# A chunked mLSTM with two gated feed-forward layers: the first 24 feed-forward steps in an order that the program fixes on all engines

## The chip, the core and the metric

The kernel runs on one core of a Trainium2 chip. Such a core has a matrix engine (TensorE, PE in the rows; its weight loads are the rows PEld), three engines for elementwise work (VectorE = DVE, ScalarE = ACT, GpSimd = POOL), and SyncE (SP), which here only starts DMA transfers. Each engine works through its own queue in order and waits for others by semaphores. The metric is device time in microseconds of one launch. All times of single instructions come from one profiled execution.

## The reference

```python
# attention: B=2, H=8, S=768, D=40; a recurrence over t
m_new = max(f[t] + m, i[t])
C = exp(f[t] + m - m_new) * C + exp(i[t] - m_new) * outer(v[t], k[t])
n = exp(f[t] + m - m_new) * n + exp(i[t] - m_new) * k[t]
y[t] = sigmoid(o_gate[t]) * (C @ q[t]) / max(|n . q[t]|, 1)

# layer 1, tokens = 1536, d_model = 320, d_ff = 1536
x = (sigmoid(x @ w_gate) * (x @ w_val)) @ w_out
# layer 2
xn = x / sqrt(mean(x*x) + 1e-6) * rms_g
out = (silu(xn @ w_gate2) * (xn @ w_val2)) @ w_out2
```

All inputs are float32.

## The kernel before

The sequence is cut into six chunks of 128 time steps. A chunk holds 128 tokens of each of the two batch entries, that is 256 tokens of layer 1. Within a chunk the recurrence is written as matrix products (scores `a_s`, decayed scores `a_p`, their product with v `a_pv`, the part from the state of the chunk before `a_inter`, the new state `a_u`, normalisation `a_h`); `a_x` transposes the result into `xT`, the moving operand of layer 1. Each of these is called once per batch entry or per four heads (`qd`).

The hidden width 1536 of a feed-forward layer is cut into 12 tiles `f` of 128. A step of layer 1, `moe(c, f)`, makes gate and value of one tile for one chunk: 16 products of 128x256 into one PSUM bank of tag "g", a sigmoid on ACT, a product `h` on DVE. `moe_out(c, f)` multiplies `h` with the output weights and adds to the banks "o". For the chunks 0 and 1 (`NAT = 2`) these are two float32 products (the trace shows each of them as two, hence "x4"); from chunk 2 on, `h` and the output weights are split into a high and a low part, and a step takes six products. Steps are numbered from 0 here: the list `seq` has 24 steps for the chunks 0 and 1 (which chunk comes when is the string `ORDER`), then 12 for each of the chunks 2 to 5, then the steps of layer 2.

A tile of weights arrives as 64-bit words by one DMA (`load_w`) and is converted: `conv_w` does two ACT instructions (a scaling of the upper words, line 167, and a shift of the top byte, line 178), `conv_1` and `conv_2` do three DVE instructions (lines 190 and 202). `split_w` makes the high and low parts: three ACT copies (line 209), then subtractions (`sub`, line 205): the large one of 128x512 either as one DVE instruction (`go=1`) or as two POOL instructions of 128x256, a small one on POOL, and a small one of 64x128 on DVE, the function `low`. A step needs all of these parts of its tile. The output weights of the chunks 2 and later are split by `split_o`: an ACT copy, and a subtraction on POOL or DVE.

What sets the order: the code is written step by step, but only what stands before step `NPIN = 8` is pinned, which means that each engine keeps the order in which the program was written (`pin`, line 764). `early(i)` holds what is written behind the first four steps. From step 8 on, the framework's scheduler orders the instructions of each engine by its own estimates of when each can start, so that an instruction written for a later step may stand ahead of one that the current step needs. The conversions of tiles 4 to 11, the loads, the attention of chunk 2 (`C2S` gives its places, `EV2` the distances within) and `split_o` go through the table `ev`, which names the step at which each is written. Three products of a zero tile, `busy(idle, ...)` in line 753, stand ahead of step 0 only to give PE something to do.

Of the kernel before, what the change touches and what calls it, by code (L numbers as in the profile page):

```python
# [7 lines left out]
F32 = mybir.dt.float32  # L8
# [6 lines left out]
AF = mybir.ActivationFunctionType  # L15
# [52 lines left out]
@with_exitstack  # L68
def mlstm_moe_kernel(ctx, tc, gate_if, gate_s, qk, qg, tok, w1, w2, rms_g, cst, out):
    nc = tc.nc  # L70
    pool = lambda name, bufs=1, **kw: ctx.enter_context(tc.tile_pool(name=name, bufs=bufs, **kw))
    const = pool("const")
    wp = pool("w")
# [70 lines left out]
    def conv_w(f, tag="wc", lo_dve=0, both=True, sg_act=0, dve=False):  # L144

        bytes_ = wraw[f].bitcast(U8).rearrange("p (n b) -> p n b", b=8)
        top = bytes_[:, :, 3]  # L150
# [451 lines left out]
    seq += [(2, c, f) for c in range(NC // 2) for f in range(NF)]  # L602
    pos = {k: i for i, k in enumerate(seq)}

    for c in range(2, NC):
        for b in range(B):
            s0 = C2S[b] if c == 2 else 12 * (c - 1) + 6 * b + S0
            qa, qb = 2 * b, 2 * b + 1
            if True:
                at(s0 - 4, load_qk, c, b)  # L610
                at(s0 - 3, load_tok, c, b)
            d = EV2
            assert s0 + d[12] <= pos[1, c, 0]
# [12 lines left out]
            at(s0 + d[7], a_k, c, qb)
# [6 lines left out]
    at(10, lambda: nc.gpsimd.tensor_scalar(out=rmsg, in0=rmsg, scalar1=2.0 ** -16, scalar2=None, op0=ALU.mult))  # L633
    assert max(X0 + X1) <= 12
    for c in range(NC):
        for b in range(B):
            i = 2 * (c % 2) + b
            at(n1 - 12 + X0[i] if c < 2 else n1 + 12 * (c // 2 - 1) + X1[i], to_xT2w, c // 2, i, 2 * c + b)
    for f in range(NF):
        t = pos[1, 0, f]  # L640
        at(NF * NAT + f - 1, split_o, f, O1[f])
        if f >= 6:
            at(t - LW, load_w, w1, f)
        if f >= 4:
# [230 lines left out]
    def early(i):

        if i == 0:
            split_w(1, 1)
            a_s(1, 1, ("o2", "o3"))
            for qd in range(4):  # L880
                a_k(1, qd)
            a_p(1, 0)
            a_p(1, 1)
            conv_w(2)
        elif i == 1:
            a_inter(1, 0)
            load_qg(1, 1)
            load_w(w1, 4)
            split_w(2, 1)
            a_p(1, 2, p2.tile([128, 4, L], F32, tag="ft", name="p"))  # L890
            a_p(1, 3, p2.tile([128, 4, L], F32, tag="ft", name="p"))
            a_o(1, 0)
            a_o(1, 1)
            a_pv(1, 0)
            a_pv(1, 1)
            a_u(1, 0)
            conv_w(3)
            load_w(w1, 5)
        elif i == 2:
            a_h(1, 0)  # L900
            split_w(3, 1)
            a_inter(1, 1, "o2")
            a_pv(1, 2, "o3")
            a_pv(1, 3, "o3")
            a_u(1, 1, "a")
            a_x(1, 0, "a")
            a_h(1, 1)
        elif i == 3:
            a_x(1, 1, "o2")

    assert min(ev) >= 0, min(ev)
    for i in range(len(seq) + SKEW):
# [9 lines left out]
        if 0 <= i < len(seq):  # L922
# [3 lines left out]
            if i < NPIN:  # L926
                early(i)
        while 0 <= i and done < len(seq) and done <= i - (SKEW if seq[done][0] == 1 and seq[done][1] >= NAT else 1):
            layer, c, f = seq[done]
            (moe_out if layer == 1 else moe2_out)(c, f)  # L930
            done += 1
# [84 lines left out]
```

## Time and profile before

| what | before |
|---|---|
| median of 3 runs | 504.8 us (503.46 to 505.42) |
| the profiled execution | 505.04 us, span 503.2 us, mean granted clock 0.989 |
| PE busy | 485.2 us (96%) |
| DVE, ACT, POOL busy | 303.1, 222.5, 210.0 us |
| window 24 to 54 us | PE busy 26.82 of 30, DVE 26.99 |
| window 54 to 131 us | PE busy 71.57 of 77, DVE 53.99, ACT 37.72, POOL 35.48 |

Step 0 starts at 26.26 us and step 23 ends at about 131 us; the rest of the span holds the steps 24 to 107. PE's busy time counts a product that runs at half clock as busy as any other, so the granted clock has to be read beside it (column PEclk, 1.00 is the full 2.4 GHz, 0.50 is 1.2 GHz). A row of the timeline gives start, duration, engine, line, operation, output and inputs; neighbouring instructions of one kind are merged ("x16"), and since products overlap, the pace is read from the start of one row to the start of the next. In brackets stands the idle time ahead of an instruction and what ended it.

### The profile page before, as it was taken

The page shows a single profiled execution, that of the slowest core. Times are in us where ns is not written, and L with a number is a line of the kernel's source. Part 1 is how long each engine was busy: PE and PEld are TensorE (multiplying, and loading weights), DVE is VectorE, ACT ScalarE, POOL GpSimd, SP SyncE. Part 2 cuts the span into 40 slices and gives each one's busy share as a digit, 9 for nine tenths or more (in the row PEclk, how much of TensorE's full clock was granted, in tenths as well). Part 3 has the DMA queues.
Part 4 walks back from the last instruction along what each step waited for, and adds up shares of the span by engine and source line. Part 5 has one row for each costly group of instructions (what it writes and reads, how often), then busy time and mean ns, then how long its engine had stood idle before and what let it go on. Part 6 is the DMA issues. An engine that isn't in the chain of part 4 may idle for free.

```text
span 503.2 us, 8423 instructions
## 1 busy us (share of the span) xinstructions
PE 485.2 (96%) x3264; PEld 434.8 (86%) x3266; DVE 303.1 (60%) x564; ACT 222.5 (44%) x485; POOL 210.0 (42%) x238
## 2 busy tenths in 40 slices
PE   8988989899999999999999889999999999999997
PEld 5877869678899999999999778988888888888886
DVE  6899594993679586596779986622352222432223
ACT  3764653553434543455578666322252222432122
POOL 2733385451256364354249996332213222132221
PEclk9998989899999999999999999999999999999999
DMA  7763736721123232023444412000010000100001
GB/s 233 250 208 116 239 108 251 253 98 40 61 64 84 80 85 82 1 67 108 158 158 156 158 66 92 1 0 1 0 54 0 1 0 1 53 2 0 1 0 52
DMA packets 12557, 42.58 MB, mean 85 GB/s; under 512 B 1590, under 2 KB 4870, under 8 KB 12518
## 3 DMA queue, kind: packets, MB, share of 16 engines
q1 hardware_dynamic: 12278, 41.84, 24.8%
q8 instruction: 25, 0.41, 0.3%
q10 hardware_dynamic: 240, 0.22, 0.2%
q14 instruction: 14, 0.11, 0.1%
HBM read 40.05 MB, written 2.00 MB: 84 GB/s over the span
## 4 chain that ended last, share of the span: by engine, by line
PE 65%; DVE 5%; DMA 4%; POOL 3%; issue 2%; ACT 1%; POOLq 0%; ACTq 0%
PE g L804 13%; PE a L804 13%; PE o L856 12%; PE g L786 11%; PE o L831 6%; PE o L786 4%; DMA wraw<-in_w_dram 4%; PE o L828 2%; POOL h L205 1%; POOL wg L205 1%; DVE wg L205 1%; PE a L392 1%; PE a L457 1%; PE a L438 1%; PE a L470 1%
## 5 line engine op out<-in xcount | busy, mean ns | idle before, releaser
L786 PE MATMUL g<-xT,wg 128*128 128x256 f32 x912 | 131.2, 293 | 1.1 <-ACT gb L338 0.4
L786 PEld LDWEIGHTS g<-xT,wg 128*128 128x128 f32 x912 | 118.2, 193 | 7.2 <-issue 1.7
L205 POOL TENSOR_TENSOR ft<-p,fb 128x512 fp32r<-128x512 f32 x35 | 45.2, 1293 | 130.6 <-ACT fb L813 130.5
L807 DVE TENSOR_TENSOR p<-p,g 128x512 f32<-128x512 f32 x36 | 24.5, 686 | 91.0 <-ACT p L806 91.0
L205 POOL TENSOR_TENSOR h<-sig,h 128x256 fp32r<-128x256 f32 x48 | 44.9, 938 | 57.2 <-ACT h L795 56.0
L831 PE MATMUL o<-wo,h 128*128 128x320 f32 x288 | 52.0, 313 | 3.9 <-POOL h L205 3.8
L856 PE MATMUL o<-wo,fb 128*128 128x320 f32 x288 | 52.9, 310 | 0.0
L804 PE MATMUL g<-xT,wg 128*128 128x512 f32 x180 | 50.7, 393 | 0.1
L813 ACT ACTIVATE fb<-p 128x512 fp32r<-128x512 f32 (+1 forms) x37 | 22.8, 620 | 60.7 <-DVE p L812 54.5
L806 ACT ACTIVATE p<-g 128x512 f32<-128x512 f32 x36 | 21.3, 596 | 62.9 <-PE g L804 59.8
L831 PEld LDWEIGHTS o<-wo,h 128*128 128x128 f32 x288 | 43.2, 189 | 6.2 <-POOL h L205 5.1
L804 PE MATMUL a<-xT,wg 128*128 128x512 f32 x180 | 47.6, 390 | 0.0
L856 PEld LDWEIGHTS o<-wo,fb 128*128 128x128 f32 x288 | 45.6, 188 | 2.0
L804 PEld LDWEIGHTS a<-xT,wg 128*128 128x128 f32 x180 | 33.7, 188 | 6.9
L812 DVE TENSOR_TENSOR p<-p,a 128x512 f32<-128x512 f32 (+1 forms) x37 | 24.6, 671 | 22.6 <-PE a L804 22.5
L804 PEld LDWEIGHTS g<-xT,wg 128*128 128x128 f32 x180 | 32.5, 188 | 5.5 <-ACT xT L515 0.4
L828 PE MATMUL o<-wf,h 128*128 128x320 f32 x96 | 34.1, 481 | 2.9 <-DVE h L791 2.9
L786 PE MATMUL o<-xT,wg 128*128 128x256 f32 x240 | 34.7, 290 | 0.0
L788 ACT ACTIVATE sig<-g 128x256 f32<-128x256 f32 x57 | 21.5, 377 | 26.8 <-PE g L786 23.5
L205 POOL TENSOR_TENSOR wg<-wc,wg 128x256 fp32r<-128x256 f32 (+1 forms) x30 | 22.8, 771 | 24.2 <-ACT wg L209 22.4
L167 ACT ACTIVATE wraw<-wraw 128x960 f32<-128x960 f32 x23 | 25.2, 1097 | 14.1 <-DMA wraw<-in_w_dram 13.9
L856 PE MATMUL o<-wo,ft 128*128 128x320 f32 x144 | 31.4, 309 | 0.0
(258 smaller groups left out, 863.5 us busy)
## 6 DMA issues: line engine op xcount, KB each, us to landing
wraw<-in_w_dram SPq DMA_DIRECT2D x24, 960.0 KB
tok<-in_tok_dram SPq DMA_DIRECT2D x12, 488.0 KB
fb<-fd SPq DMA_DIRECT2D x16, 256.0 KB
raw<-in_qk_dram SPq DMA_DIRECT2D x24, 160.0 KB
out_dram<-xn SPq DMA_DIRECT2D x12, 160.0 KB
qg<-in_qg_dram SPq DMA_DIRECT2D x10, 180.0 KB
rmsg<-in_rms_g_dram SPq DMA_DIRECT2D x1, 160.0 KB
cs<-in_cst_dram ACTq DMA_DIRECT2D x1, 136.5 KB
```

What stands on the lines that cost most here:

```text
L167: nc.scalar.activation(out=hi.bitcast(F32), in_=hi.bitcast(F32), func=AF.Copy, scale=2.0 ** -111)
L205: eng.tensor_tensor(out=out, in0=a, in1=b, op=ALU.subtract)
L786: nc.tensor.matmul(out=g[:, m, :], lhsT=w[:, m, ws, :], rhs=x[xs // 3][:, xs % 3, :], start=(i == 0), stop=(i == 7))
L788: nc.scalar.activation(out=sg, in_=g[:, 0, :], func=AF.Sigmoid, scale=2.0 ** -8)
L804: nc.tensor.matmul(out=g[m], lhsT=w[:, m, ws, :], rhs=x[xs // 3][:, xs % 3, :], start=(i == 0), stop=(i == 7))
L806: nc.scalar.activation(out=sg, in_=g[0], func=AF.Sigmoid, scale=2.0 ** -8)
L807: nc.vector.tensor_tensor(out=sg, in0=sg, in1=g[0], op=ALU.mult)
L812: nc.vector.tensor_tensor(out=sg[:, n], in0=sg[:, n], in1=g[1][:, n], op=ALU.mult)
L813: nc.scalar.activation(out=h[0][:, n], in_=sg[:, n], func=AF.Copy)
L828: nc.tensor.matmul(out=o, lhsT=h[:, n], rhs=w, start=(f == 0), stop=(f == NF - 1))
L831: nc.tensor.matmul(out=o, lhsT=h[:, hs, n], rhs=w[:, ws, :], start=(f == 0 and i == 0), stop=(f == NF - 1 and i == 2))
L856: nc.tensor.matmul(out=o, lhsT=h[hs][:, n], rhs=w[:, ws, :], start=(f == 0 and i == 0), stop=(f == NF - 1 and i == 2))
```

## The change

`NPIN` becomes 24, so that the order of all five queues is the program's own up to step 24. What the scheduler dealt out before is now written down: two tables, `pre` and `post`, name what stands ahead of and behind the products of each step. The conversion of a tile is cut into four pieces (`tile_a`: the first ACT instruction; `tile_b`: the other one and the three on DVE, then the load of the tile two further on; `tile_c`: copies and POOL subtractions; `tile_d`: the small DVE subtraction). The large subtraction goes to POOL for all tiles but tile 1. `split_o` and the attention of chunk 3 can no longer stand ahead of step 24. The gate transposes `gates_r5b` and `gates_r5c` become one function behind step 0; the three zero products go; the shift of tile 1 moves from DVE to ACT; the scaling of `rmsg` from POOL to ACT. `moe_out` of the steps 0 to 3 stands right behind its own step.

```diff
-NPIN = 8
+NPIN = 24
-C2S = (8, 10)
+C3S = (23, 28)
-ORDER = '000011110101010101010101'
+ORDER = '000011110101010101010011'
...
-    gates_r5b()
-    idle = bank("o3")
-    busy(idle, *[512] * 3)
-    xT_dup(xT[1, 0], 0, x[:, 0], "o2", False)()
-    conv_w(1, "wc", 1, False)
+    low()
+    xT_dup(xT[1, 0], 1, x[:, 1], "o3")
     a_s(1, 0, "aa")
-    xT_dup(xT[1, 0], 1, x[:, 1], idle)
     rest()
-    gates_r5c()
-    conv_1(1)
-    conv_2(1)
-    load_w(w1, 3)
+    conv_z(1)
...
+    pre = {
+        0: [(a_p, 1, 0), (tile_b, 1), (tile_a, 2)],
+        1: [(tile_d, 1), (tile_b, 2)],
+        2: [(a_h, 1, 0), (tile_d, 2)],
+        3: [(a_h, 1, 1), (tile_d, 3)],
...
+    post = {
+        0: [(conv_z, 2), (a_p, 1, 1), (tile_c, 1, 1), (gates_r5b, "o1"), (a_s, 1, 1, ("o2", "o3")), (a_o, 1, 0), (a_o, 1, 1),
+            (a_k, 1, 0), (a_k, 1, 1), (a_k, 1, 2), (a_k, 1, 3), (a_inter, 1, 0), (load_qg, 1, 1)],
...
+        9: [(a_s, 2, 0), (tile_b, 7)],
+        10: [(tile_c, 7), (tile_a, 8), (a_p, 2, 0), (a_p, 2, 1), (load_f, 2, 2), (a_inter, 2, 0), (load_qg, 2, 1)],
...
+    for f in range(4, NF):
+        pre.setdefault(2 * f - 3, []).append((tile_d, f))
```

PE's order around the attention of chunk 2, batch entry 0. In the names `a<-raw` are the scores, `a<-cm,qg` is `a_inter`, `a<-vv,p` is `a_pv`, `g<-xT,wg` a step and `o<-wf,h` its output product. Before, from behind step 8 on:

```order
L392 MATMUL a<-raw 128x128 x8
L828 MATMUL o_747<-wf,h 128x320
L828 MATMUL o_749<-wf,h 128x320
L786 MATMUL g<-xT,wg 128x256 x16
L438 MATMUL a<-cm,qg 128x126 x2
L828 MATMUL o_559<-wf,h 128x320
L828 MATMUL o_561<-wf,h 128x320
L786 MATMUL g<-xT,wg 128x256 x16
L438 MATMUL a<-cm,qg 128x84
L828 MATMUL o_747<-wf,h 128x320
L828 MATMUL o_749<-wf,h 128x320
```

Now, from behind step 9 on:

```order
L393 MATMUL a<-raw 128x128 x8
L774 MATMUL g<-xT,wg 128x256 x16
L816 MATMUL o_737<-wf,h 128x320
L816 MATMUL o_739<-wf,h 128x320
L439 MATMUL a<-cm,qg 128x126 x2
L439 MATMUL a<-cm,qg 128x84
L774 MATMUL g<-xT,wg 128x256 x16
L816 MATMUL o_486<-wf,h 128x320
L816 MATMUL o_488<-wf,h 128x320
L462 MATMUL a<-vv,p 128x42 x8
```

`a_inter` stands one step behind the scores in both, but now behind the output product too, and in one piece.

DVE's order from the state update of chunk 1 (`C_107`) on. `r` and `x` are the normalisation `a_h`, `wg<-wc,wg 64x128` is the last piece of a tile, `h` belongs to a step. Before:

```order
L477 SCALAR_TENSOR_TENSOR C_107<-C_107,gb,a 80x84
L190 SCALAR_TENSOR_TENSOR wc<-wraw,wc 128x960
L202 SCALAR_TENSOR_TENSOR wc<-wraw,wc 128x640
L202 SCALAR_TENSOR_TENSOR wf<-wraw,wc 128x320
L791 TENSOR_TENSOR h<-sig,g 128x256
L490 TENSOR_TENSOR hs<-a,hs 128x336
L493 TENSOR_TENSOR x<-x,hs 128x320
```

Now:

```order
L478 SCALAR_TENSOR_TENSOR C_107<-C_107,gb,a 80x84
L491 TENSOR_TENSOR hs<-a,hs 128x336
L494 TENSOR_TENSOR x<-x,hs 128x320
L497 TENSOR_SCALAR r<-hs 128x8
L498 SCALAR_TENSOR_TENSOR r<-hs,r 128x8
L499 RECIPROCAL r<-r 128x8
L500 TENSOR_TENSOR x<-x,r 128x320
L208 TENSOR_TENSOR wg<-wc,wg 64x128
L779 TENSOR_TENSOR h<-sig,g 128x256
L193 SCALAR_TENSOR_TENSOR wc<-wraw,wc 128x960
```

The conversion of tile 3 went from ahead of `a_h` to behind it, and the last piece of tile 2 stands directly behind `a_h`.

POOL's order around the end of the 24 steps. `wo<-wf,wo` is `split_o`, `hs` and `wraw` split v of chunk 3, `h<-sig,h` belongs to the steps from 24 on. Before:

```order
L205 TENSOR_TENSOR wo<-wf,wo 128x320 x4
L431 TENSOR_TENSOR kk<-tok,ft 128x160 x2
L478 TENSOR_TENSOR cm<-C_107,cs 120x252
L479 TENSOR_TENSOR cm<-C_107,cs 80x84
L415 TENSOR_TENSOR vv<-tok,tg 128x336
L205 TENSOR_TENSOR wg<-wc,wg 128x256 x2
```

Now:

```order
L480 TENSOR_TENSOR cm<-C_108,cs 80x84
L831 TENSOR_TENSOR ss<-ss,mhalf 128x1 x2
L208 TENSOR_TENSOR wo<-wf,wo 128x320
L416 TENSOR_TENSOR vv<-tok,tg 128x336 x2
L432 TENSOR_TENSOR kk<-tok,ft 128x160
L208 TENSOR_TENSOR wo<-wf,wo 128x320
L208 TENSOR_TENSOR hs<-vv,wraw 128x336
```

Before, `split_o` stood among the conversions of the tiles (the `wg` behind it is a tile of the 24 steps); now all of it stands behind the last state of chunk 2.

## Rows read from the trace of the kernel before

**Rows 1.** PE's waits, 0 to 150 us: total us, times, longest.
```profile
PE o L828 <- DVE h L791: 2.9, 2, 2.3
PE a L438 <- DVE p L401: 2.0, 1, 2.0
PE a L553 <- DVE x L499: 1.7, 1, 1.7
...
PE a L470 <- DVE hs L440: 0.7, 1, 0.7
```
**Rows 2.** Busy time by window: length, PE, PEld, DVE, ACT, POOL, PEclk, DMA, GB/s.
```profile
42.00:50.00 8.00, 6.31 (x35) 4.85 (x34) 7.63 (x21) 2.81 (x5) 1.44 (x3) 0.79 0.35 124
70.00:78.00 8.00, 6.00 (x29) 5.06 (x30) 6.84 (x10) 2.43 (x7) 7.09 (x10) 0.79 0.00 0
94.00:102.00 8.00, 5.92 (x31) 4.80 (x32) 7.91 (x13) 3.98 (x7) 2.85 (x6) 0.79 0.50 179
288.00:296.00 8.00, 6.11 (x46) 5.37 (x44) 7.14 (x13) 5.01 (x12) 7.69 (x9) 1.00 0.09 37
131.00:180.00 49.00, 49.00 (x424) 46.82 (x424) 37.67 (x82) 23.46 (x60) 25.56 (x33) 1.00 0.30 87
```
**Rows 3.** PE's timeline, an undisturbed step and its output product.
```profile
119.77 2.32 PE L786 MATMUL g<-xT,wg 128*128 128x256 f32 x16
121.92 1.24 PE L828 MATMUL o<-wf,h 128*128 128x320 f32 x4
122.76 2.32 PE L786 MATMUL g<-xT,wg 128*128 128x256 f32 x16
```
**Rows 4.** PE's timeline ahead of step 0.
```profile
21.68 0.42 PE L332 MATMUL a<-cs,gs 16*128 16x16 f32 x4
...
22.57 0.59 PE L99 MATMUL o<-warm 128*128 128x512 bf16 x2 [0.16 <-issue]
...
26.26 2.51 PE L786 MATMUL g<-xT,wg 128*128 128x256 f32 x16 [0.36 <-ACT gb L338]
```
**Rows 5.** DVE's timeline: state update, then normalisation of chunk 1.
```profile
37.98 0.80 DVE L477 SCALAR_TENSOR_TENSOR C<-C,gb,a 120x126 f32<-120x126 f32 x3
...
41.89 0.49 DVE L490 TENSOR_TENSOR hs<-a,hs 128x336 f32<-128x336 f32 x1
...
43.74 0.49 DVE L499 TENSOR_TENSOR x<-x,r 128x320 f32<-128x320 f32 x1
```
**Rows 6.** DVE's timeline: the small subtraction twice, and a scan between.
```profile
52.02 0.28 DVE L205 TENSOR_TENSOR wg<-wc,wg 64x128 fp32r<-64x128 f32 x1
...
84.31 2.34 DVE L354 TENSOR_TENSOR_SCAN ft<-fb,ident 128x512 f32<-128x512 f32 x2 [2.77 <-DMA fb<-fd]
...
93.09 2.49 DVE L205 TENSOR_TENSOR wg<-wc,wg 64x128 fp32r<-64x128 f32 x1
```
**Rows 7.** POOL's timeline at the second of these.
```profile
94.03 1.93 POOL L205 TENSOR_TENSOR wg<-wc,wg 128x256 fp32r<-128x256 f32 x3
```
**Rows 8.** SP's timeline: the issue of that scan's transfers.
```profile
78.44 0.84 SPq L349 DMA_DIRECT2D fb<-fd  x2
```
**Rows 9.** ACT's timeline: one tile's copies, a sigmoid, the next tile's conversion.
```profile
58.39 1.16 ACT L209 ACTIVATE wg<-wc 128x512 fp32r<-128x512 f32 x3 [1.25 <-DVE wc L202]
59.81 0.38 ACT L788 ACTIVATE sig<-g 128x256 f32<-128x256 f32 x1 [0.25 <-PE g L786]
60.22 1.10 ACT L167 ACTIVATE wraw<-wraw 128x960 f32<-128x960 f32 x1
61.22 1.08 ACT L178 ACTIVATE wc<-wraw 128x960 int32<-128x960 uint8 x1
```
**Rows 10.** Groups by form, 26 to 131 us: count, busy us, mean ns, idle before.
```profile
L190 DVE SCALAR_TENSOR_TENSOR wc<-wraw,wc 128x960 int32<-128x960 int32 x11 | 13.5, 1231 | 3.5 <-ACT wc L178 3.4
L202 DVE SCALAR_TENSOR_TENSOR wc<-wraw,wc 128x640 int32<-128x640 int32 x11 | 11.0, 996 | 0.3
...
L205 POOL TENSOR_TENSOR wo<-wf,wo 128x320 fp32r<-128x320 f32 x8 | 9.0, 1129 | 8.8 <-ACT wo L209 8.7
```

More of the change, by code (lines that the diff above doesn't have):

```diff
@@ L172, in conv_w @@
             conv[f] = hi, c, lo
+        elif lo_dve == 3:
+            tops[f] = top
         elif lo_dve == 2:
@@ L181, in conv_w, with conv_z @@
             conv_2(f)
+    tops = {}
+    def conv_z(f):
+        nc.scalar.activation(out=conv[f][1], in_=tops.pop(f), func=AF.Copy, scale=1.0 / 32, bias=-31.0 / 64)
     def conv_1(f):
@@ L625, in mlstm_moe_kernel @@
             at(s0 + d[6], a_inter, c, b)
+            if b == 0:
+                at(s0 + d[6], load_qg, c, 1)
+            elif c < NC - 1:
+                at(s0 + d[6], load_qg, c + 1, 0)
             at(s0 + d[7], a_k, c, qb)
@@ L650, in mlstm_moe_kernel @@
         at(t, conv_w, f, W2TAG[f], L2[f], True, SG2[f])
-        assert t + 1 < 72 + f and SP < CV
+        assert t + 1 < 72 + f
         at(max(t + 1, 60 + f + SKEW + 1), split_w, f, G2[f], O2[f])
@@ L731, in mlstm_moe_kernel @@
     a_pv(0, 1, "a")
-    keep.update((0, 1, 2, 3))
+    keep.update(range(NF))
     conv_w(0, "wc", 2, False, 0, True)
@@ L871, in mlstm_moe_kernel, with ft_tile @@
     hst = {}
-    done = 0
     after = ExitStack()
[L875 to L909, printed above, removed]
+    def ft_tile():
+        return p2.tile([128, 4, L], F32, tag="ft", name="p")
@@ new lines, in tile_a, with tile_b, tile_c, tile_d @@
+    def tile_a(f):
+        conv_w(f, "wc", 3, False)
+    def tile_b(f):
+        if f in tops:
+            conv_z(f)
+        conv_1(f)
+        conv_2(f)
+        if f + 2 < NF:
+            load_w(w1, f + 2)
+    lows = {}
+    def tile_c(f, go=0):
+        lows[f] = split_w(f, go, 0, False)
+    def tile_d(f):
+        lows.pop(f)()
+    pre = {
[3 more added lines that the diff above has]
+        3: [(a_h, 1, 1), (tile_d, 3)],
+        4: [(tile_b, 4)],
+    }
@@ new lines, in mlstm_moe_kernel @@
+    post = {
+        0: [(conv_z, 2), (a_p, 1, 1), (tile_c, 1, 1), (gates_r5b, "o1"), (a_s, 1, 1, ("o2", "o3")), (a_o, 1, 0), (a_o, 1, 1),
+            (a_k, 1, 0), (a_k, 1, 1), (a_k, 1, 2), (a_k, 1, 3), (a_inter, 1, 0), (load_qg, 1, 1)],
+        1: [(a_p, 1, 2, ft_tile), (a_p, 1, 3, ft_tile), (tile_c, 2), (a_pv, 1, 0), (a_pv, 1, 1), (tile_a, 3), (conv_z, 3), (a_u, 1, 0)],
+        2: [(tile_b, 3), (tile_c, 3), (a_inter, 1, 1, "o2"), (load_qg, 2, 0), (a_pv, 1, 2, "o3"), (a_pv, 1, 3, "o3"), (a_u, 1, 1), (a_x, 1, 0)],
+        3: [(a_x, 1, 1, "o2"), (tile_a, 4), (conv_z, 4)],
+        4: [(lambda: p.tensor_copy(out=ident4, in_=ident.unsqueeze(1).to_broadcast([128, 4, L])),), (load_qk, 2, 0), (load_tok, 2, 0, False), (tile_c, 4), (tile_a, 5)],
+        5: [(tile_b, 5), (load_f, 2, 0)],
+        6: [(tile_c, 5), (tile_a, 6), (load_f, 2, 1), (load_qk, 2, 1), (a_v, 2, 0)],
+        7: [(tile_b, 6), (load_tok, 2, 1, False)],
+        8: [(tile_c, 6), (tile_a, 7), (a_f, 2, 0), (a_f, 2, 1), (a_k, 2, 0), (a_k, 2, 1)],
+        9: [(a_s, 2, 0), (tile_b, 7)],
+        10: [(tile_c, 7), (tile_a, 8), (a_p, 2, 0), (a_p, 2, 1), (load_f, 2, 2), (a_inter, 2, 0), (load_qg, 2, 1)],
+        11: [(a_pv, 2, 0), (a_pv, 2, 1), (a_o, 2, 0), (a_o, 2, 1), (tile_b, 8), (a_v, 2, 1)],
+        12: [(tile_c, 8), (tile_a, 9), (a_u, 2, 0), (a_f, 2, 2), (a_k, 2, 2), (load_f, 2, 3)],
+        13: [(tile_b, 9)],
+        14: [(tile_c, 9), (tile_a, 10), (a_h, 2, 0)],
+        15: [(tile_b, 10)],
+        16: [(tile_c, 10), (tile_a, 11), (a_f, 2, 3), (a_k, 2, 3)],
+        17: [(a_s, 2, 1), (tile_b, 11)],
+        18: [(tile_c, 11), (a_p, 2, 2), (a_p, 2, 3), (a_inter, 2, 1), (load_qg, 3, 0)],
+        19: [(lambda: nc.scalar.activation(out=rmsg, in_=rmsg, func=AF.Copy, scale=2.0 ** -16),), (a_pv, 2, 2), (a_pv, 2, 3)],
+        20: [(a_u, 2, 1), (a_h, 2, 1)],
+        21: [(a_x, 2, 0)],
+        22: [(a_x, 2, 1)],
+    }
@@ L911, in mlstm_moe_kernel, with do, out_steps @@
+    for f in range(4, NF):
+        pre.setdefault(2 * f - 3, []).append((tile_d, f))
+    def do(todo):
+        for fn, *args in todo:
+            fn(*(x() if x is ft_tile else x for x in args))
+    def out_steps(i):
+        nonlocal done
+        while 0 <= i and done < len(seq) and done <= i - (0 if done < 4 else SKEW if seq[done][0] == 1 and seq[done][1] >= NAT else 1):
+            layer, c, f = seq[done]
+            (moe_out if layer == 1 else moe2_out)(c, f)
+            done += 1
     assert min(ev) >= 0, min(ev)
@@ L925, in mlstm_moe_kernel @@
             (moe if layer == 1 else moe2)(c, f)
[L926 to L931, printed above, removed]
+        if i >= 4:
+            out_steps(i)
+        do(post.get(i, ()))
+        out_steps(i)
     after.close()
```

56 lines of the change are left out of this document (21 added, 35 removed).

## The prediction

> **What bounds the kernel now.** I read the waits of PE first, then PE's busy time by window beside the granted clock, then the timelines of the engines that PE waited for. PE is the bound: it is busy 96% of the span, so only time in which PE stands still, or runs at half clock, can be won. In the first 150 us the list of PE's waits has three long entries, 2.3, 2.0 and 1.7 us, each for DVE, and some short ones; the row on `h` holds 2.9 us in two waits, the longer one 2.3 [rows 1]. The windows around the three long ones show a second cost: the granted clock has a mean of 0.79 over 8 us [rows 2], and as the clock knows two levels, 1.2 and 2.4 GHz, that is some 3.4 us at half rate around each. A wait does not always bring it: in the window 288 to 296 us PE stood still for 1.89 us in all, and the clock stayed at 1.00 [rows 2]. Between 131 and 180 us PE is busy all 49 us at full clock [rows 2]. So what the change can win lies in the first 24 steps. An undisturbed step takes 2.15 us for its 16 products and 0.84 us for its output product, 2.99 us together, from start to start [rows 3].
>
> **What is removed.** I count from the profiled execution's 505.04 us; the median of the runs shown is 504.8, 0.2 us below it, less than any term is known to.
> - The three long waits: 2.3 + 2.0 + 1.7 = 6.0 us [rows 1]. The longest comes from DVE's queue: `h` stood behind pieces of later tiles that the scheduler had put ahead of it. In the new order each tile's pieces are dealt out three to four steps ahead of its use.
> - The clock around them: 3 x 8 x (1 - 0.79) = 5.0 us [rows 2].
> - Short waits: 2.9 - 2.3 = 0.6, and 0.7 [rows 1]; 1.3 us.
> - Ahead of step 0 the waits of 0.16 and 0.36 us go [rows 4], 0.5 us. The gate transposes, from 21.68 to shortly before 22.57 us [rows 4], only move behind step 0.
>
> Together 12.8 us, so 492.2 us is the most that this can give without anything new in its place.
>
> **What comes in its place.** With all queues fixed, a wait that the scheduler filled with other work stands open. I went through the new order of each engine with durations from the rows.
> - Step 1: ACT now has the scaling of tile 2, 1.10 us [rows 9], ahead of the copies of tile 1, and it empties the gate transposes last, whose bank is that of an output product. The trace shows no such wait. It costs from 0 (the gate work and the scores lie behind step 0 on PE) to the 1.1 us that were put ahead. I take 0.8, as both engines behind it, DVE and PE, have little left to do by then.
> - Step 2: DVE has, behind the state update, the whole of `a_h` and then the last piece of tile 2. From the end of PE's `a_u` that is 0.80 for the update, 43.74 + 0.49 - 41.89 = 2.34 for `a_h` [rows 5] and 0.28 for the piece [rows 6], 3.4 us. PE has an output product and four of 16 products to do meanwhile, 0.84 + 0.54 = 1.4 us [rows 3]. So PE waits up to 2.0 us in the middle of the step. I take 1.6, since `a_h` in rows 5 is merged with gaps; from 1.2 to 2.0.
> - Step 3: the same for batch entry 1. The transposition of entry 0 and its evacuation lie on both sides of the comparison, PE and DVE. I take 1.8, from 1.2 to 3 if POOL is beside it.
> - `a_inter` of chunk 2 needs p, which stands on DVE behind two scans, a conversion and `h` of step 10. The scans wait for transfers: before, such a pair was issued at 78.44 and its scans began at 84.31 [rows 6, 8], 5.9 us later. Now a pair is issued behind the load of tile 7, two steps of 2.99 ahead of its scans, so these begin at the end of step 9 at the earliest. That makes p about 1.0 us late; from 0 to 2.3, the length of the scans [rows 6].
> - The clock: two of these waits are about as long as one that cost it (1.7) and the one that did not (at most 1.89). I take one drop, 5.0 / 3 = 1.7 us; from none to three, 5.0.
> - Behind step 24: `split_o` could run ahead before. Now eight POOL subtractions, 9.0 us [rows 10], and four on DVE stand among the steps 24 to 35, with chunk 3's attention. In that stretch POOL was busy 25.56 of 49 us [rows 2]; 34.6 of 49 now, which still leaves it a third idle. I take 0.3 us; from 0 to 6 (the second rival).
>
> Sum: 0.8 + 1.6 + 1.8 + 1.0 + 1.7 + 0.3 = 7.2; 505.04 - 12.8 + 7.2 = 499.4. Merged rows hide short waits too: step 0 took 2.51 us by its row [rows 4], an undisturbed one 2.32 [rows 3], 0.2 us, and I count that twice, for the steps 0 and 1. The forecast is 499.0.
>
> Edits that I cost at nothing: the shift of tile 1 goes from DVE to ACT, `rmsg` from POOL to ACT, the copy for the scans moves on POOL, and the 24 steps end with two of each chunk. ACT is busy 37.72 and POOL 35.48 of the 77 us of the table above, so idle time covers them; without it each would cost its own 1 us once.
>
> **A row and a rule on POOL.** The small subtraction took 0.28 us at one place and 2.49 us at 93.09 [rows 6], where POOL was in subtractions from 94.03 to 95.96 [rows 7]; PE's longest wait ended right behind it. The change adds ten of POOL's large subtractions to the 24 steps. The Trainium skill (SBUF — State Buffer, Who interferes with whom) states that a DVE instruction with two SBUF inputs and a GpSimd instruction that reads SBUF exclude each other, each for the whole of an instruction. By that rule the trace agrees, with 2.49 us for work of 0.28, and the sum would be that of the first rival; by the place of the instructions alone it stays at 499.
>
> **The rivals.**
> 1. POOL holds up DVE where PE waits: the small subtraction takes 2.5 instead of 0.3 us [rows 6] in the steps 2 and 3, 2 x 2.2 = 4.4 us, 503.4. For it: the row at 93.09, and more work on POOL. Against: for the tiles 2 and 3, POOL gets its work while DVE is still in the state update and `a_h`, and should be nearly through.
> 2. The first 24 steps win and the next 12 give it back, as POOL and DVE have `split_o` and chunk 3 at once. DVE was busy 37.67 of 49 us there [rows 2], 77%; two scans of 1.2 us [rows 6] that stood ahead of step 24 before, and four subtractions, make it about 86%. In the window at 288 us, with DVE at 7.14 and POOL at 7.69 of 8, PE lost 1.89 of 8 us [rows 2]. Half of that rate over 49 us is 5.8 us: 499.0 - 0.3 + 5.8 = 504.5. Against: POOL is at 71%, not at 96% as there.
> 3. No new wait is long: ACT and DVE keep up, the clock stays up. Then steps 1 to 3 and `a_inter` cost half of what I took, 2.6 us, and nothing else: 505.04 - 12.8 - 0.4 + 2.6 = 494.4. For it: in the early steps DVE is rid of a shift and two large subtractions.
> 4. Slower: the conversion becomes a ring that sets the pace. DVE's conversion of a tile (1.23 + 1.00 [rows 10]) waits for ACT's shift, ACT's copies (1.16) wait for DVE, and behind them ACT has the next scaling (1.10), a sigmoid (0.38) and the shift (1.08) [rows 9], 5.95 us in all. PE needs 5.98 for the two steps that use a tile and about 1.2 for attention (the table's window of 77 us, less 19 steps of 2.99 and the 9 us lost there, leaves 11 us for 9.5 pairs), 7.2. If POOL adds 2.2 us to each turn of the ring, it takes 8.2, and from that point on PE loses 1 us at each of the seven tiles 5 to 11; with the clock down around half of these waits, 3.5 x 1.7 = 6, it is 499 + 7 + 6 = 512. Against: the small subtraction and the attention on DVE lie beside ACT's part of the ring, not in it.
>
> **How the numbers follow.** Forecast 499.0, with 496.5 to 501.5 as its own range: 0.50. No long new wait, 494.4: 0.18. POOL holds up DVE, 503.4: 0.10. The steps from 24 on give it back, 504.5: 0.12. The ring, 512: 0.10. Under 0.5%, 2.5 us, is about what a measurement of this kernel cannot tell from none. Faster by more than that: 0.50 + 0.18 + 0.06 from the lower ends of the two middle cases, 0.74; within: 0.16; slower: 0.10. The range leaves out the ring and the best tenth of the third rival: 492.5 to 504.
>
> **What would show it.** Right: in the first 150 us PE has no wait for `h` or x of over 1 us; the windows 70 to 78 and 94 to 102 us show a clock of 1.00; the steps 2 and 3 show a wait for the small subtraction of 1.2 to 2 us each, and `a_inter` of chunk 2 one for p of about 1 us; step 23 ends 5 to 8 us before 131 us, and the rest keeps its length. If the small subtraction takes over 2 us in the steps 2 and 3, the first rival holds; if PE waits for POOL's `h` between the steps 24 and 36, the second; if DVE is busy without a gap in the steps 9 to 21 and PE's waits come once per tile, the fourth. I am wrong in the whole if PE's waits and half-clock time in the first 24 steps come to the 12 us of before.

## The result and the profile after

The changed kernel takes 510.97 us (median of 4 runs, 510.02 to 512.4), the kernel before 504.13 us beside it; the ratio is 1.0135 (1.0101 to 1.0169). It is slower by 1.35%, where 499.0 us, faster, was forecast, and 511 lies outside the range of 492.5 to 504. The profiled execution took 512.4 us, its span is 510.6 us, the mean granted clock 0.989, as before. Some executions, of the kernel before too, took from 514 to 1198 us; all medians and ratios from here on leave them out.

PE's waits from 0 to 150 us of the changed kernel (total us, times, longest) answer to [rows 1]:

```profile
PE g L774 <- DVE wg L208: 5.2, 2, 3.0
PE o L335 <- ACT tg L336: 5.1, 1, 5.1
PE a L439 <- issue: 1.7, 2, 1.1
...
PE o L554 <- DVE r L509: 0.5, 1, 0.5
PE g L774 <- POOL wg L208: 0.4, 1, 0.4
```

The waits for `h` and x of [rows 1] are gone, as forecast; the one of `a_inter` (L439) is still there, listed as issue (see below). In place of the others stand a wait of 5.1 us that was not among the terms, and two for the last piece of a tile (`wg`). The windows, with the columns of [rows 2]:

```profile
28.00:38.00 10.00, 5.69 (x31) 4.98 (x32) 2.36 (x5) 4.79 (x11) 2.16 (x5) 0.68 0.32 105
54.00:62.00 8.00, 4.86 (x24) 3.62 (x25) 4.44 (x9) 1.56 (x3) 2.53 (x5) 0.81 0.31 123
70.00:78.00 8.00, 8.00 (x55) 7.15 (x54) 5.79 (x11) 4.99 (x11) 2.60 (x4) 1.00 0.93 307
94.00:102.00 8.00, 8.00 (x59) 7.36 (x59) 7.46 (x12) 4.97 (x9) 6.54 (x8) 1.00 0.46 157
131.00:180.00 49.00, 47.59 (x392) 43.97 (x392) 37.92 (x75) 25.73 (x67) 33.67 (x43) 1.00 0.25 80
```

The two windows that [rows 2] shows at a clock of 0.79 are now at 1.00, with PE busy all 8 us: the fixed order does in the steps 4 to 23 what it was said to do. But 28 to 38 us has 4.3 us of idle time at a mean clock of 0.68, 54 to 62 us has 3.1 us at 0.81, and 131 to 180 us, without a gap before, has 1.4 us.

Where the 5.1 us come from needs three timelines of the changed kernel, first PE's:

```profile
24.34 2.17 PE L774 MATMUL g<-xT,wg 128*128 128x256 f32 x16
26.45 0.41 PE L335 MATMUL o<-cs,gs 16*128 16x16 f32 x4
31.98 0.71 PE L335 MATMUL o<-cs,er 16*128 16x16 f32 x5 [5.12 <-ACT tg L336]
33.02 0.60 PE L338 MATMUL o<-el,selg 16*120 16x30 f32 x2 [0.33 <-ACT te L336]
...
38.56 2.31 PE L774 MATMUL g<-xT,wg 128*128 128x256 f32 x16
```

ACT's:

```profile
28.36 1.08 ACT L163 ACTIVATE wraw<-wraw 128x960 f32<-128x960 f32 x1 [3.52 <-DMA wraw<-in_w_dram]
29.31 0.39 ACT L776 ACTIVATE sig<-g 128x256 f32<-128x256 f32 x1
29.57 1.07 ACT L184 ACTIVATE wc<-wraw 128x960 int32<-128x960 uint8 x1
30.52 1.16 ACT L212 ACTIVATE wg<-wc 128x512 fp32r<-128x512 f32 x3
31.70 0.22 ACT L336 ACTIVATE tg<-o 128x64 f32<-128x64 f32 x1
```

and DVE's:

```profile
33.66 0.42 DVE L779 TENSOR_TENSOR h<-sig,g 128x256 f32<-128x256 f32 x1 [5.85 <-PE o L338]
```

`gates_r5b` now puts four transposes (`gs`), five transposes (`er`) and a product into one bank, and ACT empties the first part (`tg`) before PE writes the second. The parts don't overlap, yet PE waits. ACT comes to `tg` at 31.70, as it stood 3.52 us for the load of tile 2, whose scaling is written ahead of the sigmoid of step 0. Behind the gate product PE goes on without a gap, with scores, `a_inter` and the output product of step 0, up to step 1 at 38.56. `h` of step 0, with its sigmoid ready at 29.7, begins only at 33.66, behind the gate product too: the program frees the gate tiles just before it opens the pool of `h`, so that `h` seems to lie in their place (read from the code, not tried). But PE has no wait for it; what delays step 1 is PE's own wait. The Trainium skill (PSUM — Partial Sum Buffer, PSUM bank collisions raise a hardware error) asks that two engines be kept apart by bank and not by address. The trace agrees in that the program keeps them apart so, with 5.12 us of waiting between disjoint columns; no run here shows what would happen without the wait.

The steps 2 and 3 on PE, changed kernel:

```profile
43.94 0.87 PE L774 MATMUL g<-xT,wg 128*128 128x256 f32 x4
47.00 1.70 PE L774 MATMUL g<-xT,wg 128*128 128x256 f32 x12 [2.18 <-DVE wg L208]
...
54.14 0.62 PE L774 MATMUL g<-xT,wg 128*128 128x256 f32 x3 [0.43 <-POOL wg L208]
57.76 1.95 PE L774 MATMUL g<-xT,wg 128*128 128x256 f32 x12 [3.00 <-DVE wg L208]
```

They are the waits forecast for these places, 2.18 for 1.6 us and 3.43 for 1.8.

`a_inter` of chunk 2, batch entry 0, on PE, and p on DVE:

```profile
85.11 0.87 PE L439 MATMUL a<-cm,qg 120*128 120x126 f32 x6 [1.11 <-issue]
84.33 1.28 DVE L402 TENSOR_TENSOR p<-a,ft 128x512 f32<-128x512 f32 x2
```

The row of DVE holds two instructions, of which the first ends at 85.01; `a_inter` begins 0.1 us behind it, and so it does for batch entry 1 (114.12 and 114.22, a wait of 0.60 us). So these look like waits for p, though the trace names no engine.

### The profile page after: what moved, and what is told of

It is laid out like the page before. It is cut to its first block, busy times and chain, and to the rows that moved or that the text cites. A ratio compares the mean times of both kernels' runs of the same rounds, so it can differ in the third digit from the quotient of the medians.

```text
span 510.6 us, 8398 instructions
## 1 busy us (share of the span) xinstructions
PE 485.4 (95%) x3263; PEld 433.9 (85%) x3263; DVE 301.2 (59%) x558; ACT 222.5 (44%) x487; POOL 210.4 (41%) x247
## 4 chain that ended last, share of the span: by engine, by line
PE 75%; DVE 9%; DMA 7%; ACT 4%; issue 3%; POOL 1%; SPq 0%; POOLq 0%; ACTq 0%; DVEq 0%
PE g L774 16%; PE g L792 13%; PE a L792 13%; PE o L844 12%; DMA wraw<-in_w_dram 6%; PE o L819 5%; PE o L816 5%; PE o L774 3%; PE a L393 1%; PE o L393 1%; PE a L439 1%; PE a L462 1%; DVE wg L208 1%; POOL h L208 1%; ACT wg L212 1%
## 5 line engine op out<-in xcount | busy, mean ns | idle before, releaser
L774 PE MATMUL g<-xT,wg 128*128 128x256 f32 x912 | 128.5, 290 | 6.2 <-DVE wg L208 5.2
L774 PEld LDWEIGHTS g<-xT,wg 128*128 128x128 f32 x912 | 116.2, 191 | 11.0 <-issue 3.7
L819 PE MATMUL o<-wo,h 128*128 128x320 f32 x288 | 53.2, 315 | 4.2 <-POOL h L208 3.8
L208 POOL TENSOR_TENSOR wg<-wc,wg 128x256 fp32r<-128x256 f32 (+1 forms) x40 | 29.9, 760 | 57.8 <-ACT wg L212 46.3
L792 PEld LDWEIGHTS g<-xT,wg 128*128 128x128 f32 x180 | 32.5, 188 | 5.5 <-ACT xT L516 0.4
L783 ACT ACTIVATE h<-sig 128x256 fp32r<-128x256 f32 x48 | 19.9, 414 | 28.1 <-DVE sig L781 27.9
L816 PE MATMUL o<-wf,h 128*128 128x320 f32 x96 | 31.6, 453 | 0.0
```

Source lines behind the costliest of these rows:

```text
L208: eng.tensor_tensor(out=out, in0=a, in1=b, op=ALU.subtract)
L774: nc.tensor.matmul(out=g[:, m, :], lhsT=w[:, m, ws, :], rhs=x[xs // 3][:, xs % 3, :], start=(i == 0), stop=(i == 7))
L792: nc.tensor.matmul(out=g[m], lhsT=w[:, m, ws, :], rhs=x[xs // 3][:, xs % 3, :], start=(i == 0), stop=(i == 7))
L816: nc.tensor.matmul(out=o, lhsT=h[:, n], rhs=w, start=(f == 0), stop=(f == NF - 1))
L819: nc.tensor.matmul(out=o, lhsT=h[:, hs, n], rhs=w[:, ws, :], start=(f == 0 and i == 0), stop=(f == NF - 1 and i == 2))
```

## The experiments

Each time is a median; the ratio, with its 95% interval, is to runs of the kernel before beside it on the same chip. The numbers 6, 7 and 12 ran once each, for their profiles.

| kernel | us | ratio to before |
|---|---|---|
| the changed kernel | 510.97 | 1.0135 (1.0101 to 1.0169) |
| 1: PE's gate work in one piece | 505.55 | 1.0016 (0.9992 to 1.0040) |
| 2: tile 2 later on ACT | 509.75 | 1.0090 (1.0062 to 1.0118) |
| 3: both | 505.27 | 0.9993 (0.9964 to 1.0022) |
| 4: both, last piece first | 499.76 | 0.9897 (0.9856 to 0.9939) |
| 9: last piece first, alone | 506.49 | 1.0034 (1.0008 to 1.0060) |
| 5: as 4, `split_o` dealt out | 499.78 | 0.9888 (0.9852 to 0.9925) |
| 10: as 4, `split_o` on POOL | 499.14 | 0.9890 (0.9867 to 0.9914) |
| 8: as 4, chunk 3 earlier | 500.80 | 0.9917 (0.9892 to 0.9942) |
| 11: as 10, tile 3 on DVE | 498.44 | 0.9874 (0.9838 to 0.9910) |

**1. PE's gate work in one piece.**

```diff
             for c in range(n):
                 nc.tensor.transpose(out=ps[:, o + U * c:o + U * c + U], ...)
-            nc.scalar.activation(out=t[:, 0:U * n], in_=ps[:, o:o + U * n], func=AF.Copy)
+            todo.append((t, n, o))
             o += U * n
         nc.tensor.matmul(out=ps[0:120, o:o + 30], lhsT=selg, rhs=el, start=True, stop=True)
+        for t, n, k in todo:
+            nc.scalar.activation(out=t[:, 0:U * n], in_=ps[:, k:k + U * n], func=AF.Copy)
```

> Edit: the nine gate transposes and the selg product follow one another on PE, and ACT's three evacuations stand behind them; all else as in the changed kernel. Theory A (PE's waits of 5.12 and 0.30 us between the transposes come from evacuations that stand between them in PE's program on one bank; h of step 0 waits for the last reader of the gate tiles, so the whole of PE stands behind ACT's wait for tile 2): both waits go, h(0) at about 29.7 instead of 33.66 us, step 1 at about 32 instead of 38.56, no 6.8 us stretch of half clock there: about 504. Rival B (the cause is only ACT's wait of 3.5 us for the load of tile 2; the order on the bank is incidental): sigmoid, copies and large subtraction of tile 1 still stand behind that wait, so step 1 moves by under 2 us: 508 to 511. Rival C (the time is found again later, as the next tiles are no earlier): step 1 is earlier, step 4 is not: 509 to 511.

505.55 us, 1.5 above theory A's number and under the ranges of B and C. PE's timeline:

```profile
27.05 0.41 PE L335 MATMUL o<-cs,gs 16*128 16x16 f32 x4
27.32 0.45 PE L335 MATMUL o<-cs,er 16*128 16x16 f32 x5
27.63 0.37 PE L338 MATMUL o<-el,selg 16*120 16x30 f32 x2
...
31.22 2.32 PE L776 MATMUL g<-xT,wg 128*128 128x256 f32 x16
```

Both waits are gone, and step 1 starts at 31.22 instead of 38.56 us; a new wait of 0.32 us, of the output product of step 0 for the last evacuation (`gb`), is all that is left. Rival B (under 2 us) falls, and so does rival C: step 4 starts at 55.88 instead of 62.44. In this execution the load of tile 2 also came sooner (ACT waited 1.44 instead of 3.52 us), which has nothing to do with the edit; number 9 below has both apart. The half clock did not go, though; it moved to the steps 2 and 3, see below.

**2. Tile 2 later on ACT.**

```diff
-        0: [(a_p, 1, 0), (tile_b, 1), (tile_a, 2)],
+        0: [(a_p, 1, 0), (tile_b, 1)],
-        0: [(conv_z, 2), (a_p, 1, 1), (tile_c, 1, 1), (gates_r5b, "o1"), ...
+        0: [(a_p, 1, 1), (tile_c, 1, 1), (gates_r5b, "o1"), (tile_a, 2), (conv_z, 2), ...
```

> Edit: the two ACT instructions of tile 2 (scaling, shift) stand behind the gate work of step 0 instead of ahead of the sigmoid of step 0; the gate work itself keeps its waits on one bank. Theory A: ACT's wait of 3.5 us for tile 2 no longer stands ahead of sigmoid, copies and the tg evacuation, so tg is emptied at about 28.2 instead of 31.7; PE still waits for it, about 1.6 us, and step 1 starts at about 32 to 33: 504 to 506. Rival B: the whole loss goes with ACT's wait, step 1 at about 30: 502. Rival C: tile 2 is now 1.2 us later, so step 2 waits longer and the gain is lost: 508 to 511.

509.75 us, 4 us above what theory A gave, so a miss in size. In the profile PE still waits for `tg`, 2.04 instead of 5.12 us, as A said; step 1 starts at 35.50, not 32 to 33, as it had half clock on the way. Rival B (all of the loss goes) falls. Rival C has the number but not the mechanism: step 2 waits 2.19 us, no longer than the 2.18 of the changed kernel.

**3. Both.** The two edits together.

> Edit: both edits, PE's gate work in one piece and tile 2's ACT instructions behind it. Theory A: sigmoid of step 0 at 26.7, copies of tile 1 until 28.2, h(0) at about 27.2, step 1 at about 30.1 instead of 38.56, clock full there: 502 to 503; steps 2 and 3 still wait 2 to 3 us each for the last piece of their tile. Rival B: no better than the later tile 2 alone. Rival C: step 2 then waits for tile 2's copies and POOL subtractions (landed at 28.3, ready at about 37), so it starts at 35 to 36 instead of 43.94 but waits 3 us or more: 504 to 506.

505.27 us, 2 to 3 above theory A's number and inside rival C's. By the profile, which is that of the fastest of the ten executions (502.79 us), step 1 starts at 30.19, as A said, at full clock, and step 2 waits 2.38, not the 3 us of rival C. The first edit alone gives as much: with PE's work in one piece, no difference can be told from where tile 2 stands on ACT.

**4. The last piece ahead of `a_h`.**

```diff
-        2: [(a_h, 1, 0), (tile_d, 2)],
-        3: [(a_h, 1, 1), (tile_d, 3)],
+        2: [(tile_d, 2), (a_h, 1, 0)],
+        3: [(tile_d, 3), (a_h, 1, 1)],
```

> Edit: as the kernel with both edits, and the small DVE subtraction (last piece) of tiles 2 and 3 stands ahead of the normalisation a_h instead of behind it. Theory A: the waits of 2.18 and 3.00 us of steps 2 and 3 for the last piece go too, and with them the 3.4 us of half clock at 57.8 us: 5.2 + 1.7 = 6.9 us less than the kernel with both edits, about 495 to 496. Rival (steps 2 and 3 then wait for POOL's subtractions of the same tile or for x of a_h one step later): 1 to 3 us of it come back, 497 to 499. If the last piece was not what steps 2 and 3 waited for: same as the kernel with both edits.

499.76 us, 5.5 below kernel 3 and 0.8 above the rival's 497 to 499. PE's timeline in the steps 2 and 3 and behind them:

```profile
37.07 1.70 PE L776 MATMUL g<-xT,wg 128*128 128x256 f32 x12 [0.22 <-DVE wg L208]
...
44.21 2.05 PE L776 MATMUL g<-xT,wg 128*128 128x256 f32 x15 [0.43 <-POOL wg L208]
47.81 0.41 PE L556 MATMUL o<-cs,x 128*128 128x128 f32 x2 [1.54 <-DVE x L502]
```

The waits of 2.38 and 3.00 us fell to 0.22 and none; 1.54 us came back as a wait for x, as the rival said.

**9. The same edit on the changed kernel alone.**

> Edit on the changed kernel alone (511.0): the last piece of tiles 2 and 3 ahead of a_h; gate order and tile 2's ACT instructions as in the changed kernel. Theory A (independent losses): step 1 stays as late as in the changed kernel, but the 2.18 and 3.00 us at steps 2 and 3 go as they did with both gate edits (505.3 to 499.8, 5.5 us): 505 to 507. Rival (the small subtraction's place is worth less while step 1 is late, since the wait then falls on x and on POOL): 508 to 510.

506.49 us, theory A. In ratios it takes 0.0101 off the changed kernel, the edits to the gate work (numbers 1 and 3) 0.0119 and 0.0142, all together 0.0238: the two losses add up.

This kernel still has the gate work as the changed kernel has it, and in its profile the load of tile 2 came nearly as soon as in that of number 1. PE and ACT here, and then ACT in number 1:

```profile
30.56 0.71 PE L335 MATMUL o<-cs,er 16*128 16x16 f32 x5 [3.62 <-ACT tg L336]
30.28 0.22 ACT L336 ACTIVATE tg<-o 128x64 f32<-128x64 f32 x1
30.32 0.23 ACT L340 ACTIVATE tg<-o 128x64 f32<-128x64 f32 x1
```

ACT comes to `tg` at the same time in both. PE waits 3.62 us for it here and not at all in number 1, and step 1 starts at 37.25 against 31.22. So PE's wait comes from the order on the bank, and ACT's lateness sets its length.

**5, 6, 8, 10 and 12. Behind step 24.** Number 5 deals nine of the `split_o` out to the steps 9 to 23, 6 and 10 move its four DVE subtractions to POOL, 8 and 12 put chunk 3's attention back to the steps 20 and 26, all on kernel 4:

```diff
+EARLY = {0: 9, 1: 11, 2: 13, 3: 15, 4: 17, 5: 19, 6: 21, 7: 22, 8: 23}
+    for f, i in EARLY.items():
+        post.setdefault(i, []).append((split_o, f, O1[f]))
...
-O1 = (0, 0, 0, 0, 0, 0, 1, 0, 1, 1, 0, 1)
+O1 = (0, 0, 0, 0, 0, 0, 0, 0, 0, 0, 0, 0)
...
-C3S = (23, 28)
+C3S = (20, 26)
```

> Edit on the best kernel so far (both gate edits and the last piece first, 499.8): split_o of the tiles 0 to 8 is written behind the steps 9, 11, 13, 15, 17, 19, 21, 22 and 23 instead of 23 to 31, an ACT copy and a subtraction each. Theory (second rival in small: behind step 24, split_o and chunk 3's attention load DVE and POOL at once, so PE waits 0.55 us for wc and 0.86 us for x): in 131 to 180 us PE's idle time falls from 1.42 us to 0.5 or less, and the steps 9 to 23 have room for it: 498.4 to 499. Counter-theory (the 24 steps have no room: POOL subtractions of 1.13 us and ACT copies stand ahead of pieces of tiles): new waits of 1 us or more between steps 9 and 23: 500 to 502.

> Edit on the best kernel so far: the four split_o subtractions of DVE (0.48 us each) go to POOL, places unchanged. If DVE's load by split_o makes x and wc late, PE's waits of 0.55 and 0.86 us in 131 to 180 us shrink by a half or more (up to 1.9 us less on DVE). If it is chunk 3's late place, both stay within 0.2 us. Time by itself: within 1 us of 499.

> Edit on the best kernel so far: chunk 3's attention is placed at the steps 20 and 26 instead of 23 and 28, as before the change, split_o stays behind step 24. If chunk 3's late place causes PE's 1.42 us of idle time in 131 to 180 us, it falls to under 0.5 us: 498.4 to 499. If split_o causes it, the wait for wc or x stays within 0.3 us of 0.55 and 0.86. Counter-theory: chunk 3's scans and conversions (1.2 and 0.8 us on DVE each) now stand among the last tiles, and PE waits there 1 us or more: 500 to 502.

> The kernel with both gate edits, the last piece first and all of split_o's subtractions on POOL, timed: by its profile PE's idle time in 131 to 180 us was 0.88 instead of 1.42 us, so about 0.5 us below 499.8: 498.5 to 499.8, which a comparison with the kernel before cannot tell from the one without this edit.

> The kernel with chunk 3's attention at the steps 20 and 26, again, for its profile (timed: 501.7, 500.0 to 504.6). If chunk 3's late place caused PE's idle time of 1.42 us in 131 to 180 us, it is under 0.5 us here; what made it about 2 us slower than the kernel without this edit stands as waits of PE in 95 to 131 us, for p, wc or wg on DVE.

Busy time by window, with the columns of [rows 2], first kernel 4:

```profile
80.00:131.00 51.00, 50.41 (x358) 44.06 (x358) 33.39 (x65) 23.37 (x54) 25.50 (x34) 1.00 0.36 115
131.00:180.00 49.00, 47.58 (x418) 45.04 (x417) 41.85 (x86) 24.91 (x62) 29.25 (x37) 1.00 0.30 92
```

kernel 5:

```profile
80.00:131.00 51.00, 49.16 (x346) 42.61 (x345) 36.44 (x66) 25.21 (x59) 29.00 (x35) 1.00 0.35 111
131.00:180.00 49.00, 49.00 (x429) 46.59 (x429) 39.30 (x87) 23.36 (x57) 27.56 (x36) 1.00 0.33 95
```

kernel 12:

```profile
80.00:131.00 51.00, 47.60 (x345) 41.80 (x345) 34.88 (x66) 22.75 (x48) 19.16 (x27) 0.97 0.35 109
131.00:180.00 49.00, 48.55 (x423) 46.08 (x421) 40.22 (x92) 26.09 (x69) 36.54 (x45) 1.00 0.33 98
```

Kernel 4 loses 1.42 us behind 131 us. With `split_o` dealt out that goes to zero, and 1.25 us more are lost ahead of it; the time stays. With chunk 3 earlier it falls to 0.45, and 2.8 us more are lost ahead, 2.2 of them in one wait (`a_s` of chunk 3 for the evacuation of `xT` on DVE), and the clock falls there too. Its median is 500.80 us (number 8), 1.0 above kernel 4 and not the 2 us that the expectation of number 12 starts from; the execution profiled as number 12 took 499.70. With all of `split_o` on POOL 0.85 to 0.88 is left (498.48 and 499.14 us); a comparison cannot tell that from kernel 4. So the wait behind step 24 is real, and `split_o` takes part in it, but the same work is only moved: no placement tried was worth over 1 us.

The loss there is larger than these waits. The steps 23 to 35, from the start of step 23 to that of step 36, before and in the changed kernel:

```profile
128.75:176.26 47.51, 47.51 (x409) 45.23 (x408) 35.56 (x81) 22.89 (x59) 23.32 (x32) 1.00 0.26 77
130.79:181.92 51.13, 49.72 (x407) 46.10 (x406) 39.84 (x78) 27.15 (x70) 34.28 (x44) 1.00 0.27 86
```

They take 3.6 us longer, at full clock in both. Only 1.4 of it is idle time; PE's busy time grew by 2.2 us, for nearly the same number of products. Kernel 5, without any idle time there, still takes 49.5 us. The order in which PE's products of chunk 3 stand among those of the steps is another one; whether that makes them longer no run tried.

**7 and 11. POOL beside DVE.** Tile 3's large subtraction goes from POOL to DVE, in number 7 on kernel 3, in number 11 on kernel 10 and behind the state update:

```diff
-        2: [(tile_b, 3), (tile_c, 3), (a_inter, 1, 1, "o2"), ... (a_u, 1, 1), (a_x, 1, 0)],
+        2: [(tile_b, 3), (a_inter, 1, 1, "o2"), ... (a_u, 1, 1), (tile_c, 3, 1), (a_x, 1, 0)],
```

Number 7 only writes `(tile_c, 3, 1)` for `(tile_c, 3)`.

> Edit on the kernel with both gate edits (505.3), where step 3 waits 0.43 us for POOL and 3.00 us for the last piece: the large subtraction of tile 3 goes from POOL (two instructions of about 0.95 us) to DVE (one of 0.68). First rival (POOL beside DVE stretches a_h of entry 1: x 0.87, r 0.64 and 0.83 us against 0.49, 0.33 and 0.17 where POOL is idle): a_h of entry 1 takes about 2.4 us instead of 3.6 from its first to its last instruction, and the wait in the middle of step 3 falls to about 2 us (DVE's own 0.68 stands earlier). If the stretch has another cause, a_h keeps 3.6 us.

> As the kernel timed beside it, and the large subtraction of tile 3 on DVE, written behind the state update of chunk 1, entry 1. POOL is then free during a_h of entry 1: that goes from 3.3 us to about 2.4, x for a_x comes about 0.8 us sooner (1.6 us wait of PE falls to about 0.8), and step 3's wait of 0.43 us for POOL goes: 0.8 to 1.2 us below the kernel beside it, 497.5 to 498.5. If the stretch of a_h has another cause than POOL, DVE is 0.7 us later and PE waits 2.2 us for x: 499.5 to 500.5.

Number 7 (503.55 us) doesn't tell the theories apart: PE was at half clock until about 52 us, so that `a_h` came late and POOL was through in any case; in kernel 1, which leaves the subtraction on POOL, `a_h` took the same 2.08 us for that reason. Number 11's profiled execution took 513.76 us and stood at half clock too, but until about 43 us; it met this place, some 15 us later than the others, at full clock. DVE's timeline of `a_h` of entry 1, first kernel 3:

```profile
45.93 0.50 DVE L493 TENSOR_TENSOR hs<-o,hs 128x336 f32<-128x336 f32 x1
46.46 0.87 DVE L496 TENSOR_TENSOR x<-x,hs 128x320 f32<-128x320 f32 x1
47.25 0.64 DVE L499 TENSOR_SCALAR r<-hs 128x8 f32<-128x8 f32 x1
47.93 0.83 DVE L500 SCALAR_TENSOR_TENSOR r<-hs,r 128x8 f32<-128x8 f32 x1
...
49.53 0.28 DVE L208 TENSOR_TENSOR wg<-wc,wg 64x128 fp32r<-64x128 f32 x1
```

kernel 11:

```profile
59.94 0.51 DVE L493 TENSOR_TENSOR hs<-o,hs 128x336 f32<-128x336 f32 x1
60.48 0.53 DVE L496 TENSOR_TENSOR x<-x,hs 128x320 f32<-128x320 f32 x1
60.94 0.58 DVE L499 TENSOR_SCALAR r<-hs 128x8 f32<-128x8 f32 x1
61.55 0.17 DVE L500 SCALAR_TENSOR_TENSOR r<-hs,r 128x8 f32<-128x8 f32 x1
...
62.40 0.41 DVE L781 TENSOR_TENSOR h<-sig,g 128x256 f32<-128x256 f32 x1
```

`a_h` takes 2.46 instead of 3.60 us, PE's wait for x falls from 1.6 (kernel 10) to 0.91 us, and the one for POOL is gone: in the places the theory holds. The time, 498.44 against 499.14, lies in the theory's range, but the intervals of the two ratios overlap, so it decides nothing.

## Why the prediction was wrong

The step that failed is the first of "what comes in its place": step 1, put at 0.8 us with bounds 0 to 1.1, where PE waited 5.45 us. Another is the last of them, behind step 24, put at 0.3 us: from step 23 on, the profiles of the changed kernel and of the kernels 1, 3, 4 and 6 are 3.5 to 5.4 us longer than before. The terms against the changed kernel's rows:

| term | forecast, us | measured, us |
|---|---|---|
| step 1 | 0.8 | 5.12 + 0.33 = 5.45 |
| step 2 | 1.6 | 2.18 |
| step 3 | 1.8 | 0.43 + 3.00 = 3.43 |
| `a_inter` of chunk 2 | 1.0 | 1.7, two waits put down to issue |
| the clock | 1.7 | 10 x 0.32 + 8 x 0.19 = 4.7 |
| behind step 24 | 0.3 | 49 - 47.59 = 1.4 of idle time |
| sum | 7.2 | 18.9 |

499.4 + 18.9 - 7.2 = 511.1, within 1.3 us of the profiled 512.4. Part of that is chance. For the first 24 steps the terms give 17.5 - 12.8 = 4.7 us more than before, but step 23 starts only 2.0 us later (130.79 against 128.75). From there to the end of the span it is 510.6 - 130.79 = 379.8 us against 503.2 - 128.75 = 374.4, 5.4 more, where the table counts the 1.4 of idle time.

- **Step 1** was bounded by the length of what was put ahead on ACT. Two things were missed. The scaling of tile 2 is not only 1.1 us long, it waits for a load, and everything behind it on ACT waits too. And on PE the second set of transposes stands behind an evacuation of the first, since both use one bank; so ACT's lateness becomes PE's own, and with it that of step 1. The wait that the term did name, of an output product for the bank that is emptied late, does not occur; in kernel 1 it is 0.32 us. The kernels 1 and 9 show that the order on the bank is what decides; kernel 2, that ACT's lateness sets how long it lasts.
- **The clock** was the second miss, 4.7 for 1.7. Its larger part, 3.2 us, lies around the wait of step 1. So the 5.0 us that went at the three old places came back at two new ones.
- **Steps 2 and 3** were the right mechanism (kernels 4 and 9), with step 3 too small: `a_h` took 3.60 us there, not 2.34. That is the first rival's mechanism at another place than I looked: the small subtraction itself took 0.28 us, but `a_h` ahead of it was stretched beside POOL.
- **`a_inter`** was, as far as the trace shows, right in kind, and in size for batch entry 0 (1.11 for 1.0); the 0.60 us of entry 1 were not counted.
- **Behind step 24** was far too small, 0.3 for 5.4. That is the size of the second rival (5.8), without its sign: PE waits for wc and x on DVE there, 1.4 us, not for POOL's `h`, and most of the loss is no wait.
- Of the rivals, the ring has the time (512) and not the mechanism: PE waits nowhere at the tiles 5 to 11 for a piece of a tile. That its number fits is chance.
- "Wrong in the whole" was tied to 12 us of waits and half clock in the first 24 steps; there were 17.5.

With the three edits the time is the forecast one: 499.76 us against the 499.0, and 1.0% under the kernel before. That is no merit of the sum, whose terms for the steps 1 to 3 those edits removed. Step 23 starts at 118.67 us there, 10.1 earlier than before, where 5 to 8 were forecast, and from it to the end 4.1 us are lost again (497.2 - 118.67 = 378.5), where 0.3 were.

That kernel 2 is so much worse than kernel 3 can be read from the profiles (508.65 and 502.79 us): from the first gate transposes to step 1 it takes 8.91 us against 3.58, of which 2.37 are its waits on the bank and about 3 the half clock behind them.

Left open: which waits cost the clock, and why PE's busy time in the steps 23 to 35 grew.

## What to carry to other kernels

Where an order is fixed by hand, follow each engine's queue through what it waits for, not only through how long its instructions take: one instruction that waits for a load stops everything written behind it. Where several small PE results share a bank, write all of PE's work first and the evacuations behind it. Put the small piece that the next step waits for ahead of a long chain that nobody needs yet; here that alone was worth 1%.

## What the runs showed of the hardware

- Waits of nearly the same length cost the clock or not. The window 24 to 54 us of kernel 1, with a longest wait of 2.30 us, and that of kernel 3, with 2.38 and 3.00:

```profile
24.00:54.00 30.00, 26.77 (x183) 23.48 (x183) 20.87 (x43) 11.73 (x24) 11.83 (x20) 0.83 0.43 156
```

```profile
24.00:54.00 30.00, 24.07 (x186) 20.37 (x183) 22.93 (x45) 12.92 (x27) 10.58 (x19) 0.96 0.44 153
```

  By that the first lost 30 x 0.17 = 5.1 us to half clock and the second 1.2, and PE's idle time differs the other way. So a term for the clock needs a range of some 4 us. Ten runs of kernel 3 spread as much, from 502.79 to 507.65 us, but that is not shown to be the clock: the slowest had a mean of 0.990, one of 503.41 us had 0.986.
- POOL beside DVE stretches even tiny instructions: `r` of 128x8 took 0.64 us in kernel 3 and the one behind it 0.83; in kernel 1, where POOL was idle then, both took 0.17. The Trainium skill (SBUF — State Buffer, Who interferes with whom) has a DVE instruction with at most one SBUF input run free of GpSimd outside some fast modes. The first of these two has one input and was stretched; whether it ran in such a mode no run here shows.
- The same load takes its time unevenly. ACT's wait for tile 2 ended 7.7 us after the load was issued in the changed kernel (20.69 to 28.36), 6.1 in kernel 9 (20.87 to 26.93) and 5.6 in kernel 1 (21.32 to 26.91). An order fixed by hand has to bear each of these.
